# Output projection of an attention and MLP kernel: from full-array matmuls to two 64-row tiles, with new banks clearing and new queue orders

## The chip, the core and the metric

One NeuronCore of a Trainium2 chip. It has a matrix engine (TensorE, here PE), three elementwise engines (VectorE or DVE, ScalarE or ACT, GpSimd or POOL), a queue that issues transfers (SyncE or SP), on-chip memory of 128 partitions, and eight accumulator banks that only PE writes by matmul. Each engine takes its own instructions in order and waits on semaphores for the others. The metric is the device time of one execution, in microseconds (us); lower is better.

## The reference

Two layers, each an attention block A and an MLP block B on a sequence of 2048 tokens with 576 features; the same weights serve both layers. Cut to what matters:

```python
def _A_ref(x, wqkv, wo):            # H = 32 heads of Dh = 18, window W = 256
    q, k, v = split_heads(x @ wqkv)
    scores = einsum("bhqd,bhkd->bhqk", q, k) * Dh ** -0.5
    p = softmax(where(causal_and_within_W, scores, -1e9))
    o = einsum("bhqk,bhkd->bhqd", p, v)
    return merge_heads(o) @ wo      # the output projection, 576 x 576

def _B_ref(x, w1, b1, w2, b2):      # F = 4608
    h = gelu(layernorm(x) @ w1 + b1)
    return h @ w2 + b2

x = x + _A_ref(layernorm(x), wqkv, wo)
x = x + _B_ref(layernorm(x), w1, b1, w2, b2)
# and both once more
```

## The kernel before

**Tiling.** The two layers are cut into eight chunks of four token tiles (128 tokens each), four chunks a layer; `k` counts chunks from 0. For a chunk, PE runs: QKV (`qkv`, L842), scores (`scores`, L921, matmuls at L932), probabilities times values (`pv`, L966, matmuls at L978), the output projection (`tail`, L1051), the first MLP matmul (`G_part`, L1073, matmuls at L1098) and the second (`mm2`, L1120). ACT does the exponentials (L941) and the gelu (L1108), POOL the masks (L961), DVE the copies out of the banks, the layer-norm statistics (L719) and the residual adds (L1041). Work of neighbouring chunks is interleaved.

**Order.** Every piece of work is a task made by `add`, numbered in the order in which the program makes it. The order of the tasks on each of the five queues is not computed at build time: it is written out in the table `ORDER` (one string of task numbers for each engine), and the bank of every accumulator in the string `BANKS`. `Plan.schedule` walks through these strings with a cost for every task and puts in the waits; its one choice is to fill PE's gaps in the first 140 us with dummy matmuls (`keep_warm`, `warm_fn` at L709). The constant `SWITCH` is its cost for a change of array mode.

**Array shapes.** Every PE task has a mode. "f" uses the whole array. "r" (scores) uses four tiles of 32 rows. "c" uses either the whole array or four tiles of 32 columns (`quad`, L802: line 804 is the whole array, line 807 the four column tiles); `Plan.schedule` takes the column tiles where the task stands next to `pv`, which always uses them. "h" (QKV from the third chunk on, L863, and `G_part`) uses two tiles of 64 rows that write two different banks. An "h" task pair works in two phases: in the first, rows 0 to 63 write bank 0 and rows 64 to 127 write bank 1; in the second the halves change banks. Because both halves then add to what the other half wrote, the second phase is marked `own` and waits for PE's own count of the first. In the last of five pieces of features (`c == 4`, 64 features) QKV needs only the first phase, so the phases have ten and eight matmuls.

**Attention output.** Heads are kept in four groups of eight, one group in every 32 partitions; after `pv`, DVE transposes the result into `oq` (L989), divides by the sum into `attq` (L992, L995) and transposes `attq` into `attT` (L999) in five pieces of 32 columns, with task names `aT0` to `aT4`. A head group has 8 x 18 = 144 features, so pieces 0 to 3 hold 32 features of each group and piece 4 holds 16 features and 16 zeros. The zeros come from a POOL memset of `attq` (`aqd`) and a DVE memset of piece 4 of `wo_sb`.

**Output projection.** `tail` makes for each token tile two tasks by `two_out` (L811), one for each half of 288 output columns; each takes a bank and runs five matmuls, one for each piece, with `attT` against `wo_sb`. `resid` then adds each bank to the residual stream (L1041), and the layer norm for the MLP follows.

**Start and weights.** SP loads two tiles of x (`xin`), the weights of q (`wqA`, `wqB0`, `wqB1`), those of k and two more tiles of x. PE clears the eight banks by matmuls of a zeroed tile `warm` (`zero`, L697, L700), transposes the first tiles (L761) and starts on QKV of chunk 0 (L823). `wo_load` (L1202) issues four loads of 128 rows (`woA`) and four of 16 rows (`woB`).

Of the kernel before, what the change touches and what calls it, by code (L numbers as in the profile page):

```python
# [348 lines left out]
SWITCH = 0.103  # L349
# [4 lines left out]
def spread(s):  # L354
    for x in s.split():
# [178 lines left out]
def build_kernel(nc, A_x, A_wqkv, A_wo, B_x, B_w1, B_b1, B_w2, B_b2, out):  # L534
# [96 lines left out]
    def mm_cost(n):  # L631
        return n / 2400.0 + 0.0023
# [706 lines left out]
```

## Time and profile before

| | |
|---|---|
| Runs, median (lowest to highest of 3) | 860.43 us (859.88 to 860.76) |
| The profiled execution's own time | 860.22 us |
| Its span, first to last instruction | 858.5 us |
| Granted clock of PE over the span | 1.00 |
| Bytes read from HBM | 90.10 MB, 108 GB/s over the span |

The profile is one execution. "Busy" is the time in which an engine has at least one instruction running, "idle before" the time that an engine stood still just before the instructions of a group, with what ended it. A group is all instructions of one source line, engine and operation; `x` stands ahead of their number. A timeline merges neighbours of one group and gives the start, the length, and the group. Matmuls overlap: a new one starts before the last has ended, so a rate is read from start to start.

### The profile page before, as it was taken

Reading aid. Unit: us, or ns where it says so; the run is one execution under the profiler, and the core shown is the slowest. Engines: PE = TensorE matmul, PEld = TensorE weight load, DVE = VectorE, ACT = ScalarE, POOL = GpSimd, SP = SyncE. Lnnn points to the kernel's source line nnn. Section 1 sums busy time; section 2 is a strip of 40 time slices with the busy share of each in tenths; the row PEclk is TensorE's granted clock in tenths of the full one; section 3 lists DMA queues with packets and bytes.
Section 4 is the critical chain, followed back from the end, with each engine's and each line's share of the span. In section 5 each row is a group of like instructions: output and inputs, shape, how many; then the busy total and the mean of one; then the engine's idle time right before and its main releaser. Section 6 shows DMA issues by size and latency. Waiting matters only on the chain.

```text
span 858.5 us, 26755 instructions
## 1 busy us (share of the span) xinstructions
PE 846.7 (99%) x11500; PEld 521.2 (61%) x11500; DVE 384.8 (45%) x934; ACT 596.1 (69%) x741; POOL 371.3 (43%) x560
## 2 busy tenths in 40 slices
PE   8999999999999999999999999999999999999998
PEld 6555556656556566566566666756656656656556
DVE  6788234545237533373255632663325424243013
ACT  4986887868767788477755887548777689762730
POOL 3766644565235563156330672424634265421200
PEclk9999999999999999999999999999999999999999
DMA  7495763472575721956348626475444773535620
GB/s 210 75 164 118 225 184 92 123 197 55 161 177 120 157 75 61 209 145 173 94 133 205 164 63 211 69 162 146 133 131 91 157 226 100 161 128 141 232 84 28
DMA packets 181862, 119.77 MB, mean 140 GB/s; under 512 B 107440, under 2 KB 181744, under 8 KB 181744
## 3 DMA queue, kind: packets, MB, share of 16 engines
q1 hardware_dynamic: 181744, 118.05, 53.0%
q8 instruction: 91, 1.49, 0.7%
q14 instruction: 27, 0.22, 0.1%
HBM read 90.10 MB, written 2.36 MB: 108 GB/s over the span
## 4 chain that ended last, share of the span: by engine, by line
PE 93%; ACT 2%; issue 1%; DMA 1%; DVE 1%; POOL 1%; SPq 0%
PE ps L1098 33%; PE ps L804 30%; PE ps L863 10%; PE ps L807 8%; PE ps L932 6%; PE ps L978 5%; ACT pT L941 2%; PE ps L823 1%; POOL pT L961 1%; DMA wqkv<-in_A_wqkv_dram 1%; DMA xnTm<-xn 0%; SPq L659 0%; ACT hT L1108 0%; DVE oq L989 0%; DVE xn L744 0%
## 5 line engine op out<-in xcount | busy, mean ns | idle before, releaser
L941 ACT ACTIVATE pT<-ps 128x1024 bf16<-128x1024 f32 (+1 forms) x384 | 346.5, 972 | 62.4 <-PE ps L932 61.7
L961 POOL TENSOR_SCALAR_AFFINE_SELECT pT<-pT 128x512 bf16<-128x512 bf16 (+1 forms) x368 | 280.3, 785 | 238.7 <-ACT pT L941 233.9
L1098 PE MATMUL ps<-xnTm,w_sb 64*128 64x512 bf16 x2592 | 291.2, 376 | 1.4 <-DMA xnTm<-xn 0.5
L1108 ACT ACTIVATE hT<-ps,b1col 128x512 bf16<-128x512 f32 x276 | 169.5, 687 | 162.2 <-PE ps L1098 161.8
L1098 PEld LDWEIGHTS ps<-xnTm,w_sb 64*128 64x128 bf16 x2592 | 130.1, 94 | 141.1 <-issue 7.6
L804 PE MATMUL ps<-w_sb,hT 128*128 128x288 bf16 x1542 | 205.8, 287 | 0.0
L1041 DVE TENSOR_TENSOR x_res<-ps,x_res 128x288 f32<-128x288 f32 x224 | 98.3, 449 | 181.0 <-PE ps L804 159.1
L804 PEld LDWEIGHTS ps<-w_sb,hT 128*128 128x128 bf16 x1542 | 143.5, 98 | 52.2 <-issue 15.2
L863 PE MATMUL ps<-wqkv,xnTa 64*128 64x288 bf16 x1296 | 92.2, 283 | 0.9 <-DVE x_res L1041 0.3
L884 DVE CAST qn<-ps 128x288 bf16<-128x288 f32 x120 | 50.8, 448 | 83.6 <-PE ps L863 78.3
L989 DVE STREAM_TRANSPOSE oq<-ps 128x512 f32<-128x512 f32 x64 | 45.7, 714 | 93.3 <-PE ps L978 92.5
L863 PEld LDWEIGHTS ps<-wqkv,xnTa 64*128 64x128 bf16 x1296 | 62.0, 94 | 30.5 <-issue 3.8
L807 PE MATMUL ps<-w_sb,hT 128*32 128x288 bf16 x2280 | 79.2, 286 | 0.0
L807 PEld LDWEIGHTS ps<-w_sb,hT 128*32 128x32 bf16 x2280 | 58.7, 97 | 11.9 <-issue 3.3
L932 PE MATMUL ps<-qT,kT 32*128 32x384 bf16 (+2 forms) x1216 | 64.1, 276 | 1.2 <-ACT pT L941 1.2
L871 DVE CAST vA<-ps 128x288 bf16<-128x288 f32 x64 | 27.5, 449 | 74.6 <-PE ps L863 71.5
L732 POOL TENSOR_SCALAR vtmp<-mv_all 128x1 f32<-128x1 f32 (+1 forms) x43 | 8.5, 199 | 113.3 <-DVE mv_all L723 110.8
L719 DVE BATCH_NORM_STATS2 st_all<-x_res 128x6 f32<-128x288 f32 (+1 forms) x128 | 54.2, 445 | 3.3 <-DMA x_res<-in_A_x_dram 2.8
L1113 POOL TENSOR_TENSOR x_res<-x_res,b2bc 128x576 f32<-128x576 f32 x32 | 40.5, 1277 | 32.7 <-ACT hT L1108 32.7
L978 PE MATMUL ps<-pT,vA 128*20 128x384 bf16 (+2 forms) x1408 | 50.4, 276 | 0.8 <-DVE vA L871 0.6
L932 PEld LDWEIGHTS ps<-qT,kT 32*128 32x128 bf16 x1216 | 19.3, 92 | 41.7 <-issue 27.6
L804 PE MATMUL ps<-wo_sb,attT 128*128 128x288 bf16 x320 | 43.1, 287 | 0.2 <-issue 0.2
(56 smaller groups left out, 460.3 us busy)
## 6 DMA issues: line engine op xcount, KB each, us to landing
w_sb<-in_B_w_dram SPq DMA_DIRECT2D x46, 864.0 KB, 5.5
w_sb<-in_B_w_dram SPq DMA_DIRECT2D x48, 768.0 KB, 5.6
w_sb<-in_B_w_dram SPq DMA_DIRECT2D x96, 48.0 KB, 3.4
wqkv<-in_A_wqkv_dram SPq DMA_DIRECT2D x3, 576.0 KB, 5.4
x_res<-in_A_x_dram SPq DMA_DIRECT2D x3, 576.0 KB, 5.8
wqkv<-in_B_w_dram SPq DMA_DIRECT2D x2, 864.0 KB, 5.1
out_dram<-x_res SPq DMA_DIRECT2D x12, 144.0 KB, 3.2
wo_sb<-in_A_wo_dram SPq DMA_DIRECT2D x4, 144.0 KB, 2.6
```

What stands on the lines that cost most here:

```text
L719: add("dve", lambda e, i=i, s=s: e.bn_stats(st_all[:, t, i, :], s[:, t, i * HB:(i + 1) * HB]), reads=res, writes=[f"st{t}_{i}"], cost=0.37 ...
L804: return e.matmul(bank(b)[:, 0:HB], lhs, rhs, start=start, stop=stop, skip_group_check=True)
L807: ins = e.matmul(bank(b)[32 * j:32 * j + 32, 0:HB], lhs[:, 32 * j:32 * j + 32], rhs, start=start, stop=stop, tile_position=(0, 32 * j), sk ...
L863: ins = e.matmul(bank(bs[o])[:, 0:HB], xnTa[r:r + 64, c, i * 128:(i + 1) * 128], wqkv[r:r + 64, c, col:col + HB], start=(c == 4), stop=(ph ...
L884: add("dve", lambda e, b=bs[o], dst=dst: e.tensor_copy(dst, heads_of(bank(b))), reads=[bs[o]], writes=[f"qn{sl}h{o}"], cost=0.375, lat=0.1 ...
L932: ins = e.matmul(two(bs[j // 2])[:, j % 2, col:col + nq * 128], k_of(T0 + so)[0][32 * j:32 * j + 32, g, :], qs[32 * j:32 * j + 32, g, qo * ...
L941: add("act", lambda e, h2=h2: e.activation(pT[:, sl, 2 * h2:2 * h2 + 2, lo:hi], two(bs[h2])[:, :, lo:hi], ACT.Exp, scale=SCALE), reads=[bs ...
L961: add("pool", lambda e, ap=ap, pat=pat, sgn=sgn, kind=kind: e.affine_select(ap, ap, pattern=pat, compare_op=(ALU.is_ge if kind == "d" else ...
L978: ins = e.matmul(bank(bo)[32 * j:32 * j + VW, qo * 128:(qo + nq) * 128], vA[:, (T0 + so) % VS, 8 * j + g, :], pT[:, sl, j, col:col + nq * ...
L1041: add("dve", lambda e: e.tensor_tensor(x_res[:, t, sl], bank(b)[:, 0:HB], x_old[:, t, sl], ALU.add), reads=[b] + ([f"xin{t}"] if first els ...
L1098: ins = e.matmul(bank(bks[i])[:, 0:n], w1_sb[r:r + 64, sls[i], col:col + 128], xnTm[r:r + 64, k % 2, c, 0:n], start=(c == 4), stop=(ph == ...
L1108: add("act", lambda e, ff=ff, hd=hd, bk=bk: e.activation(hd[:, 0:n], bank(bk)[:, 0:n], ACT.Gelu_apprx_tanh, bias=b1col[:, ff:ff + 1]), rea ...
```

## The change

- **Projection.** `tail` makes for each token tile two tasks of mode "h" with two banks: ten matmuls in the first phase, then eight with `own`, each of 64 rows.
- **Packing.** After the last head group of a chunk, two DVE copies (`ax0`, `ax1`) write columns 128 to 143 of partitions 0 to 63 into columns 144 to 159 of partitions 64 to 127, and the other way round. After the transpose, either half of piece 4 holds the last 16 features of all four groups, in 64 rows. `wo_load` puts the matching weights there: the lower 64 rows for the first 288 columns, the upper 64 for the other, by eight loads of 16 rows and 288 columns instead of four of 16 rows and 576. The two memsets for zeros go.
- **Clearing.** Eight tasks of two 256-column matmuls on the whole array become one task of 35 matmuls of 512 columns in tiles of 64 x 128, 32 x 128, 128 x 32 and 32 x 64 (rows x columns).
- **Order.** `ORDER` and `BANKS` are replaced as a whole; `SWITCH`, and the transfer rate that the planner assumes, change. The second PE transpose of a first tile now names both of its sources.

```diff
-SWITCH = 0.103
+SWITCH = 0.110
...
-        n = 2 if cls != "xr" else 4
+        n = 2
...
-        kw.setdefault("move", n / (330e3 if cls != "xr" else 165e3))
+        kw.setdefault("move", n / 280e3)
...
-    add("pool", lambda e: e.memset(attq[:, :, 8 * DH:KD * 32], 0.0), writes=["aqd"], cost=0.5, prio=-8)
...
-    add("dve", lambda e: e.memset(wo_sb[:, 4, :], 0.0), writes=[f"woB{j}" for j in range(4)], cost=0.4, prio=-8)
...
-    def zero(e, b):
+    def zero(e, bs):
+
         ins = None
-        for c in range(2):
-            ins = e.matmul(bank(b)[:, c * 256:(c + 1) * 256], warm[:, :], warm[:, :].unsqueeze(1).to_broadcast([P, 2, P]), start=True, stop=True)
+        row = [[(0, 64, 0, 0, 128), (64, 64, 1, 0, 128)]] + [[(0, 64, 0, 0, 128), (64, 32, 2, 0, 128), (96, 32, 3, 0, 128)]] * 3
+        col = [[(0, 128, 4, 64 * h, 32), (0, 128, 4, 64 * h + 32, 32)] + [(32 * j, 32, (5, 6, 7, 0)[j], 64 - 64 * h, 64) for j in range(4)] for h in (0, 1, 0, 1)]
+        for tiles in (*row, *col):
+            for r, nr, b, c, ncol in tiles:
+                ins = e.matmul(bank(bs[b])[c:c + ncol, :], warm[r:r + nr, 0:ncol], warm[r:r + nr, :].unsqueeze(1).to_broadcast([nr, 4, P]),
+                               start=True, stop=True, tile_position=(r, c), skip_group_check=True)
         return ins
-    for i in ZERO:
-        b = Bank((i,))
-        add("pe", lambda e, b=b: zero(e, b), reads=["warm"], writes=[b], cost=0.43, lat=0.2, prio=-7, alloc=[b])
+    zs = [Bank((i,)) for i in range(8)]
+    add("pe", lambda e: zero(e, zs), reads=["warm"], writes=zs, cost=3.5, lat=0.2, prio=-7, alloc=zs)
...
-                add("pe", fn, reads=rd[cs[0] // 4:][:1] + ["ident"], writes=[b], cost=0.1 * len(cs), prio=prio, alloc=[b] if cs[0] == 0 else ())
+                add("pe", fn, reads=rd[:1 + cs[0] // 4] + ["ident"], writes=[b], cost=0.1 * len(cs), prio=prio, alloc=[b] if cs[0] == 0 else ())
...
+        if g == G - 1:
+            for h in range(2):
+                add("dve", lambda e, h=h: e.tensor_copy(attq[64 - 64 * h:128 - 64 * h, 0:4 * nt, 144:160], attq[64 * h:64 * h + 64, 0:4 * nt, 128:144]),
+                    reads=[f"aq{g}"], writes=[f"ax{h}"], cost=0.33, lat=0.14, prio=prio - 3)
...
-                    reads=[f"aq{x}" for x in range(32 * c // DH, g + 1)] + ["aqd"], writes=[f"aT{c}"], cost=0.6, lat=0.14, prio=prio - 3)
+                    reads=[f"aq{x}" for x in range(32 * c // DH, g + 1)] + (["ax0", "ax1"] if c == KD - 1 else []), writes=[f"aT{c}"], cost=0.6, lat=0.14, prio=prio - 3)
...
-            bs = two_out(lambda c, i=i: attT[:, c, i * 128:(i + 1) * 128], lambda c, s: wo_sb[:, c, s:s + HB],
-                         [f"aT{c}" for c in range(KD)] + [f"wo{x}{j}" for x in "AB" for j in range(4)], prio, mode="c")
+            bs = [Bank(FILL), Bank(FILL)]
+            for ph in range(2):
+                def half(e, ph=ph, i=i, bs=bs):
+                    ins = None
+                    for c in ((4, 0, 1, 2, 3) if ph == 0 else (0, 1, 2, 3)):
+                        for o in ((0, 1) if ph == 0 else (1, 0)):
+                            r = 64 * (o ^ ph)
+                            ins = e.matmul(bank(bs[o])[:, 0:HB], attT[r:r + 64, c, i * 128:(i + 1) * 128], wo_sb[r:r + 64, c, o * HB:o * HB + HB],
+                                           start=(c == 4), stop=(ph == 1 and c == 3), tile_position=(r, 0), skip_group_check=True)
+                    return ins
+                add("pe", half, reads=[f"aT{c}" for c in range(KD)] + [f"woA{j}" for j in range(4)] + [f"woB{n}" for n in range(8)], writes=bs,
+                    cost=mm_cost(HB) * (5 - ph), lat=0.22, prio=prio, mode="h", own=(ph == 1), alloc=(bs if ph == 0 else ()))
...
-            dma("sp", wo_sb[32 * j:32 * j + 16, 4, :], A_wo[r + 128:r + 144, :], reads=["aq0"], writes=[f"woB{j}"], cls="wo", cost=0.6)
+        for n, j in enumerate((0, 2, 1, 3, 2, 0, 3, 1)):
+            r = 8 * DH * j + 128
+            cols = slice(n // 4 * HB, n // 4 * HB + HB)
+            dma("sp", wo_sb[16 * n:16 * n + 16, 4, cols], A_wo[r:r + 16, cols], reads=["aq0"], writes=[f"woB{n}"], cls="wo", cost=0.6)
```

The first task numbers of PE and SP show how far the start moves (12 on each; 0 and 1 are the first tiles of x, 2 to 4 the weights of q, 5 to 7 those of k, 8 two more tiles of x, 9 to 11 the weights of v):

```diff
 "pe":
-        "27 31 29 33 26 28 32 30 43 44 77 83
+        "24 34 35 69 68 48 49 74 73 84 58 59
...
 "sp":
-        "0 2 1 4 3 5-8 76 10 11
+        "0 2 1 6 3 8 4 7 5 67 10 9
```

In the new numbering 24 is the clearing, 34 and 35 transpose the first tile, 68 and 69 are its q, 48 and 49 transpose the second tile, 73 and 74 are the k of the first.

More of the change, by code (lines that the diff above doesn't have):

```diff
@@ L361 @@
     "pe":
[47 rows of a table removed]
-    "act":
[30 rows of a table removed]
-    "dve":
[37 rows of a table removed]
-    "pool":
[39 rows of a table removed]
[49 rows of a table added]
+    "act":
[30 rows of a table added]
+    "dve":
[38 rows of a table added]
+    "pool":
[39 rows of a table added]
 }
 BANKS = (
-        "76543210313512070747601020376160667676414240244240524627402460240240274024026402470240240250202407676676707766667677"
-        "76767571654460202020240202026042077456310275420420420472042047204213766766710264503751642042042004203076765677567544"
-        "67546754675675467625646767210654702312040020452002204202056767746765473104410320060240724020240204576435676723601137"
-        "54602402402740245766076466527574765467554752437266575675271501623546702020240624020270202547675436654712360123020240"
-        "24702402450202447676767465762305703202402406240216767752447655446572554764147757472654566066341074031020202025040202"
-        "40204764674776623017456320202024027402402340246676747667012564710320240240274024236767267314545566457704742656574556"
-        "27646076301233705202002040200424524207671667574765234076230420204270420427042076736667646230165431202020202602023573"
-        "56754747465754675754665567456202316470123560714230204204250442204202477656766770162345602302022024702402450202667456"
-        "76746570123012302400402640242573677645674764675717646574257456746747136510132467502022440642042034204176267656230176"
-        "74526042042042604204260420667766777645723016457202042027202064654765714741603675430172603511207543417203460122604753"
-        "14567301265737416531704351467230757234130")
@@ new lines @@
+        "76543210636216464741055501616364445433750226600620162626402470420422604262461264206246246242002631610100454671110150"
+        "01077742574650424020260220201624247632407163542060206042606203622637545454550324176514060026026526623254140455410767"
+        "63276657465745410415342531576405301700660060276202207242455424457616073461071020602606526022042020445547745653274106"
+        "53202620620660047454573255432767564647574745326654324763273624710754002060424704240262040757676766547362307162024204"
@@ new lines @@
+        "20640200272020167564767643012750375642464262462411710106075642121302147656420523076547632357631745310200440423024004"
+        "52020377627676107463254376064606466044040364044323222722105524376760626062610220253746445743240524352653076256043425"
+        "35342506161725741066002602260606706027532445457465321076542024246402464260422466175010164107573524104040404704040376"
+        "72761762763716076736263306532620574512174647521300242042450242027202036767647664757532641040640460046644226446133221"
@@ L534, in build_kernel @@
+        "10331205476326464246426646263010147155764304765326375216250274162505442651337417362462660504060600606643322501764253"
+        "20536124024202440200252002776577667647510327564206202624626235450544134714236517640415250157672306075433421642760651"
+        "45170643251045647106360754260431542673571")
 def build_kernel(nc, A_x, A_wqkv, A_wo, B_x, B_w1, B_b1, B_w2, B_b2, out):
@@ L617, in build_kernel @@
     OUT = (7, 6, 5, 4)
-    ZERO = (7, 6, 5, 4, 3, 2, 1, 0)
     MM1 = (0, 1, 2, 3, 4, 5, 6, 7)
```

307 rows, old and new, of the table ORDER are left out of this document.

## The prediction

> **What bounds the kernel now.** I read the page first, then the list of waits of TensorE (PE).
>
> ```profile
> span 858.5 us, 26755 instructions
> PE 846.7 (99%) x11500; PEld 521.2 (61%) x11500; DVE 384.8 (45%) x934; ACT 596.1 (69%) x741; POOL 371.3 (43%) x560
> PEclk9999999999999999999999999999999999999999
> ```
> ```profile
> PE ps L700 <- DVE warm L695: 1.6, 1, 1.6
> PE ps L823 <- DMA wqkv<-in_A_wqkv_dram: 1.6, 1, 1.6
> PE ps L932 <- ACT pT L941: 1.5, 7, 0.2
> PE ps L978 <- DVE vA L871: 0.6, 1, 0.6
> PE ps L1098 <- DMA xnTm<-xn: 0.5, 1, 0.5
> ```
>
> PE is busy for 99% of the span at full clock, and no other engine passes 69%. The five longest waits make 5.8 us; 3.2 us of them (L700, L823) lie in the first ten microseconds. So the time is the length of PE's own instruction stream plus a few waits. Columns taken off that stream shorten the kernel one for one, as long as the hand-written order leaves no new hole in it.
>
> "Busy" doesn't tell how fast PE streams, because matmuls overlap. I take rates from start to start, in the timeline of PE where the fifth chunk's QKV, first MLP matmuls and output projection follow each other (start, length, then the group):
>
> ```profile
> 459.18 0.78 PE L863 MATMUL ps<-wqkv,xnTa 64*128 64x288 bf16 x10
> 459.79 1.24 PE L1098 MATMUL ps<-xnTm,w_sb 64*128 64x512 bf16 x10
> 460.87 0.65 PE L863 MATMUL ps<-wqkv,xnTa 64*128 64x288 bf16 x8
> 461.36 1.03 PE L1098 MATMUL ps<-xnTm,w_sb 64*128 64x512 bf16 x8
> ...
> 467.63 2.62 PE L804 MATMUL ps<-wo_sb,attT 128*128 128x288 bf16 x20
> 470.19 0.40 PE L932 MATMUL ps<-qT,kT 32*128 32x384 bf16 x8
> 470.52 0.79 PE L804 MATMUL ps<-wo_sb,attT 128*128 128x288 bf16 x5
> 471.14 1.63 PE L804 MATMUL ps<-w_sb,hT 128*128 128x288 bf16 x12
> ...
> 537.98 1.52 PE L863 MATMUL ps<-wqkv,xnTa 64*128 64x288 bf16 x18
> 539.43 0.91 PE L804 MATMUL ps<-w_sb,hT 128*128 128x288 bf16 x6
> ...
> 545.84 2.38 PE L863 MATMUL ps<-wqkv,xnTa 64*128 64x288 bf16 x36
> 548.15 0.40 PE L932 MATMUL ps<-qT,kT 32*128 32x256 bf16 x8
> ```
>
> **Term 1, the projection itself.** Today five 128-row matmuls of 288 columns take 471.14 - 470.52 = 0.62 us, and two whole token tiles with one change of array shape behind them 470.19 - 467.63 = 2.56 us. With about 0.10 us for the change (next paragraph) that is 1.23 us for a tile's ten matmuls. The new form issues ten 64-row matmuls, then eight: exactly what L863 does for QKV with the same 288 columns. There ten take 459.79 - 459.18 = 0.61 us and eight 461.36 - 460.87 = 0.49 us, together 1.10 us, because two of them run at a time (a pair in 0.122 us). Ten slots become nine: 0.125 us less for each tile, and there are
>
> ```profile
> L804 PE MATMUL ps<-wo_sb,attT 128*128 128x288 bf16 x320 | 43.1, 287 | 0.2 <-issue 0.2
> ```
>
> 320 / 10 = 32 tiles: **-4.0 us**.
>
> **Term 2, changes of array shape.** The projection moves from the full array to the 64-row shape, which QKV and the first MLP matmul use. A change costs (548.15 - 545.84) - 2 x 1.10 = 0.11 us, some 0.10 us. I counted shapes along both PE order strings of the diff (task numbers shifted by the tasks that the diff adds and removes): 414 changes before, 413 after. Projection tiles sit more often next to 64-row work, but scores (32-row) are cut into it as often: **-0.1 us**.
>
> **Term 3, the second phase waits for the first.** The second eight matmuls carry the wait that QKV has (`own`): the row halves swap banks, so PE waits for its own count. Where nothing stands between the phases, QKV's eighteen take 539.43 - 537.98 = 1.45 us, less 1.10 and a change of 0.10: 0.25 us of emptying. In the new order, 6 of the 32 tiles have their phases directly behind each other; the other 26 have another matmul task in between, the shortest a score group with 0.33 us (470.52 - 470.19), which covers 0.25 us. QKV has 6 such places instead of 5. Seven times 0.25: **+1.75 us**. Queued behind each such wait is all of PE.
>
> **Term 4, the packing copies.** Two copies on DVE for each chunk, sixteen in all, each of 256 bf16 per partition on 64 partitions, stand between the last group's normalisation and the transpose of piece 4 (`aT4`), for which the first projection matmul waits. No row has this copy; the nearest are
>
> ```profile
> L884 DVE CAST qn<-ps 128x288 bf16<-128x288 f32 x120 | 50.8, 448 | 83.6 <-PE ps L863 78.3 <-PE ps L807 2.2 <-PE ps L804 2.1
> L1218 DVE CAST b1col<-ps 128x36 f32<-128x36 bf16 x1 | 0.2, 186 | 0.0
> ```
>
> so between 0.19 and 0.45 us; I take 0.32, between them, 0.64 us for the two (0.38 to 0.90). In four chunks only the PE work of 4 to 6 tasks covers that chain; the others have 5.8 us and more. The transposes beside the first projection matmul, in the first and the sixth chunk:
>
> ```profile
> 64.93 1.30 DVE L999 STREAM_TRANSPOSE attT<-attq 128x512 bf16<-128x512 bf16 x2
> 66.91 2.00 PE L804 MATMUL ps<-wo_sb,attT 128*128 128x288 bf16 x15 [0.20 <-issue]
> ...
> 554.58 1.30 DVE L999 STREAM_TRANSPOSE attT<-attq 128x512 bf16<-128x512 bf16 x2
> 556.61 1.63 PE L804 MATMUL ps<-wo_sb,attT 128*128 128x288 bf16 x12
> ```
>
> Slack from the transposes' end: 66.91 - 66.23 = 0.68 and 556.61 - 555.88 = 0.73 us, each above 0.64; the last chunk has more. In the third (k = 2) the new order takes a residual add out of the chain and puts one more score group on PE. **0 us**; at 0.90 us for a pair 0.2 us shows in each of these two chunks, and without any cover four chunks would pay 4 x 0.64 = 2.6 us.
>
> **Term 5, the start.** Rows of PE and of DVE:
>
> ```profile
> 1.63 3.37 PE L700 MATMUL ps<-warm 128*128 128x256 bf16 x16 [1.63 <-DVE warm L695]
> 5.68 0.51 PE L761 MATMUL ps<-ident,xn 128*128 128x128 bf16 x5 [0.35 <-DVE xn L744]
> 7.01 0.77 PE L823 MATMUL ps<-wqkv,xnTa 128*128 128x288 bf16 x5 [0.28 <-ACT xnTa L764]
> 9.37 1.39 PE L823 MATMUL ps<-wqkv,xnTa 128*128 128x288 bf16 x10 [1.58 <-DMA wqkv<-in_A_wqkv_dram]
> 9.85 0.82 DVE L719 BATCH_NORM_STATS2 st_all<-x_res 128x6 f32<-128x288 bf16 x2 [0.94 <-DMA x_res<-in_A_x_dram]
> ```
>
> Clearing streams 16 x 256 = 4096 columns in 3.4 us (the first matmuls run slowly). The new clearing has 35 matmuls of 512 columns, grouped so that eight groups fill the array side by side: 8 x 512 = 4096 columns, the same 3.4 us, and the first transpose waits for DVE until 5.68 anyway. After it PE now does both halves of the first q and the second transpose before the first k; the load for k is queued behind two more tiles of x. The nine loads were all in at 9.85, so k starts there instead of at 9.37 (+0.48), but 0.61 us of q and some 0.27 us of transpose are done by then: **-0.4 us**. Bounds: -0.9 (k still at 9.37) and +0.5 (nothing gained). The last weight rows come in eight small loads instead of four:
>
> ```profile
> L659 SPq DMA_DIRECT2D wo_sb<-in_A_wo_dram x8: 347/504/588, 34.4 to 62.0; - x8
> ```
>
> Four more at 0.5 us (the median of min/median/max in ns) hold up SP, and the transposes queued on it, by 2 us between 34 and 62 us; all twelve stand there ahead of the last k transpose of their stretch, while the old last one stood behind it. The two memsets that go were beside other work. Nothing booked for either.
>
> **Sum.** -4.0 - 0.1 + 1.75 - 0.4 = -2.75 us: the span of 858.5 becomes 855.75. The median of the runs, 860.43, lies 1.93 above the span (the profiled execution's own time is 860.22), so I forecast **857.7 us**. What no row prices is the search: every queue is re-sorted. I value it at 0 for the likeliest case, with -2.6 and +2.6 as bounds: the three waits of the list behind the start (1.5 + 0.6 + 0.5) all gone, or as much again.
>
> **Rivals.**
> *The new order also closes holes:* no wait after the start, 857.7 - 2.6 = **855.1**. For it: 1.5 us of PE's waits are seven small ones on the exponentials, a matter of spacing. Against it: the old order was searched too.
> *The new order opens holes:* 857.7 + 2.6 = **860.3**. For it: all queues move at once, so every cover of the old order is up for change. Against it: the list is short for 11500 matmuls, so orders with few waits can be found.
> *The mixed clearing doesn't overlap.* Nothing in the trace runs tiles of two sizes side by side. All 35 one after the other: eight at 3.4/8 = 0.42 us, then 27 at 0.216 us (460.87 - 459.79 for five) = 9.2 us, the end at 10.8; plus 1.33 us to q (7.01 - 5.68), 1.23 and 0.27, so k starts near 13.6 instead of 9.85: +3.8, **861.5**, slower than before. If only different sizes exclude each other there are 15 groups and 14 changes: 3.4 + 7 x 0.216 + 1.4 = 6.3 us, k at 10.8, +0.9: 858.6. The kernel becomes slower once clearing ends after about 9.7. [...]
> *The residual adds become the wait.* A tile now keeps two of four banks until both adds have run, and both become ready at once:
>
> ```profile
> L1041 DVE TENSOR_TENSOR x_res<-ps,x_res 128x288 f32<-128x288 f32 x224 | 98.3, 449 | 181.0 <-PE ps L804 159.1 <-PE ps L807 21.0
> L719 DVE BATCH_NORM_STATS2 st_all<-x_res 128x6 f32<-128x288 f32 x96 | 41.4, 447 | 0.4
> ```
>
> Two adds are 0.90 us, a tile on PE 1.10. One statistic of 0.45 us queued between them makes it 1.35, and the tile after next is 0.25 us late; with both, 0.70 us. It decides where it catches 4 of the 32 tiles (2.75 / 0.70); caught on one tile in five, 6.5 x 0.70 = 4.5 us: **862.2**. Against it: the order can put scores and statistics between, and DVE is idle half the time.
> *The pairs don't overlap:* 18 x 0.122 = 2.2 us a tile, +31 us, **889**. L863 has the very shape; nearly excluded.
>
> **How the numbers follow.** Forecast 0.55 (own range 856.4 to 859.2), holes closed 0.17, holes opened 0.08, clearing 0.10, adds 0.09, no overlap 0.01. Less than 0.2% (1.7 us, about what a measurement tells from nothing) is no change: faster means under 858.7, slower over 862.1. Faster: 0.48 of the forecast, 0.17 of the holes closed and 0.03 of the clearing (its smaller form), **0.68**. Same: 0.07 of the forecast, 0.08 and 0.06 of the holes opened and the clearing, **0.21**. Slower: 0.09, 0.01 and 0.01 of the adds, the clearing and no overlap, **0.11**. The range goes from 855.1 less the 0.5 of the start's lower bound, 854.6, to the clearing's 861.5; the adds, the last case and the edges stay outside.
>
> **What would show it.** Term 1: 576 matmuls of 64 rows with `wo_sb`, ten in 0.61 us. Term 3: tiles with eighteen in a row of 1.35 us. Term 4: no PE wait on `attT`. Term 5: clearing ends by 5.1 and k starts near 9.85. I am wrong if PE's list of waits grows by several microseconds, above all on DVE's adds or on ACT, or if clearing reaches past 7 us.

## The result and the profile after

The changed kernel is slower. Eight runs of each:

| | median (lowest to highest) | profiled execution: own time, span |
|---|---|---|
| before | 860.51 us (859.88 to 861.92) | 860.22, 858.5 us |
| after | 862.77 us (862.11 to 863.81) | 863.81, 862.1 us |

The ratio is 1.0026, 95% interval 1.0015 to 1.0037: +2.3 us, where -2.75 was forecast. The profiled execution is the longest of the eight, so the accounts below are made against its own span, +3.6 us.

The page of the changed kernel, its span and the busy time of the engines:

```profile
span 862.1 us, 27852 instructions
PE 848.2 (98%) x12042; PEld 517.9 (60%) x12042; DVE 387.3 (45%) x949; ACT 597.3 (69%) x741; POOL 371.4 (43%) x559
```

and its list of PE's waits (total, times, longest), the answer to the first list of the prediction:

```profile
PE ps L704 <- DVE warm L695: 2.3, 1, 2.3
PE ps L1116 <- DMA xnTm<-xn: 2.3, 3, 1.3
PE ps L936 <- issue: 1.2, 1, 1.2
PE ps L936 <- ACT pT L945: 1.0, 4, 0.3
PE ps L808 <- DVE qn L888: 0.8, 2, 0.5
PE ps L1116 <- DVE qn L888: 0.6, 1, 0.6
```

PE is still the bound, and nothing stands on the residual adds (the one row on them, L1071, has 0.2 us). But the list behind the start, all rows added and those of clearing and the first QKV left out, has grown from 4.1 to 6.8 us. The start, in the timeline of PE:

```profile
2.31 7.68 PE L704 MATMUL ps<-warm 64*128 64x512 bf16 x35 [2.31 <-DVE warm L695]
9.92 0.45 PE L765 MATMUL ps<-ident,xn 128*128 128x128 bf16 x5
...
12.70 2.00 PE L827 MATMUL ps<-wqkv,xnTa 128*128 128x288 bf16 x15
...
34.06 0.67 PE L982 MATMUL ps<-pT,vA 128*20 128x384 bf16 x16
```

Clearing takes 7.7 us instead of 3.4 and reaches to 10.0. It also starts 0.68 us later (2.31 instead of 1.63), because the new order of DVE puts the memset of `warm` behind three others (0.42, 0.17 and 0.42 us) instead of two (0.17 and 0.42). The first transpose starts at 9.92 instead of 5.68, the first k at 12.70 instead of the forecast 9.85. The first `pv` is a good mark because the whole start lies ahead of it. In the kernel before it is

```profile
32.18 0.67 PE L978 MATMUL ps<-pT,vA 128*20 128x384 bf16 x16 [0.19 <-POOL pT L961]
```

so the changed kernel is 34.06 - 32.18 = 1.9 us late there. The projection of the fifth chunk, in its timeline further on:

```profile
467.95 0.79 PE L1071 MATMUL ps<-wo_sb,attT 64*128 64x288 bf16 x10
468.56 0.67 PE L867 MATMUL ps<-wqkv,xnTa 64*128 64x288 bf16 x8
...
470.60 2.62 PE L1071 MATMUL ps<-wo_sb,attT 64*128 64x288 bf16 x36
473.15 0.40 PE L936 MATMUL ps<-qT,kT 32*128 32x384 bf16 x8
473.48 0.66 PE L1071 MATMUL ps<-wo_sb,attT 64*128 64x288 bf16 x8
474.07 0.91 PE L808 MATMUL ps<-w_sb,hT 128*128 128x288 bf16 x6
```

Ten matmuls take 468.56 - 467.95 = 0.61 us, eight with the change behind them 474.07 - 473.48 = 0.59, so 0.49: a tile is 1.10 us, as forecast. The 36 in a row take 2.55 us: two tiles, a change and one emptying of 2.55 - 2.20 - 0.10 = 0.25 us. The rows of the projection and of the packing copies among the groups (busy, mean ns | idle before):

```profile
L1071 PE MATMUL ps<-wo_sb,attT 64*128 64x288 bf16 x576 | 41.1, 283 | 0.7 <-DVE x_res L1049 0.2
L1003 DVE COPY attq<-attq 64x256 bf16<-64x256 bf16 x16 | 3.5, 222 | 0.5
```

From each start of a projection group to the start of what follows, listed idle time left out, PE spends 40.7 us on the projection before and 39.0 after, changes of shape and emptying behind its groups included.

### The profile page after: what moved, and what is told of

Its sections match the earlier page's. It is cut to its first block, busy times and chain, and to the rows that moved or that the text cites. A ratio compares the mean times of both kernels' runs of the same rounds, so it can differ in the third digit from the quotient of the medians.

```text
span 862.1 us, 27852 instructions
## 1 busy us (share of the span) xinstructions
PE 848.2 (98%) x12042; PEld 517.9 (60%) x12042; DVE 387.3 (45%) x949; ACT 597.3 (69%) x741; POOL 371.4 (43%) x559
## 4 chain that ended last, share of the span: by engine, by line
PE 92%; DMA 4%; ACT 2%; DVE 1%; issue 1%; SPq 0%; DVEq 0%
PE ps L1116 32%; PE ps L808 25%; PE ps L811 10%; PE ps L867 9%; PE ps L936 6%; PE ps L982 4%; PE ps L1071 4%; DMA xnTm<-xn 2%; ACT pT L945 1%; PE ps L827 1%; PE ps L704 1%; DMA x_res<-qn 1%; DMA kT<-qn 1%; DVE qn L888 0%; DMA xnTa<-xn 0%
## 5 line engine op out<-in xcount | busy, mean ns | idle before, releaser
L808 PE MATMUL ps<-w_sb,hT 128*128 128x288 bf16 x1452 | 193.9, 287 | 0.2 <-DVE oq L993 0.2
L808 PEld LDWEIGHTS ps<-w_sb,hT 128*128 128x128 bf16 x1452 | 134.4, 98 | 50.9 <-issue 15.2
L811 PE MATMUL ps<-w_sb,hT 128*32 128x288 bf16 x2640 | 91.7, 287 | 0.0
L811 PEld LDWEIGHTS ps<-w_sb,hT 128*32 128x32 bf16 x2640 | 67.7, 97 | 15.0 <-issue 5.3
L936 PEld LDWEIGHTS ps<-qT,kT 32*128 32x128 bf16 x1216 | 19.4, 92 | 40.7 <-issue 24.8
L1071 PE MATMUL ps<-wo_sb,attT 64*128 64x288 bf16 x576 | 41.1, 283 | 0.7 <-DVE x_res L1049 0.2
L748 DVE TENSOR_SCALAR xn<-x_res,mv_all,rstd 128x576 bf16<-128x576 f32 (+1 forms) x64 | 36.6, 578 | 10.8 <-DMA xnTm<-xn 4.3
```

Of the source, the lines that this page charges most:

```text
L808: return e.matmul(bank(b)[:, 0:HB], lhs, rhs, start=start, stop=stop, skip_group_check=True)
L811: ins = e.matmul(bank(b)[32 * j:32 * j + 32, 0:HB], lhs[:, 32 * j:32 * j + 32], rhs, start=start, stop=stop, tile_position=(0, 32 * j), sk ...
L936: ins = e.matmul(two(bs[j // 2])[:, j % 2, col:col + nq * 128], k_of(T0 + so)[0][32 * j:32 * j + 32, g, :], qs[32 * j:32 * j + 32, g, qo * ...
L1071: ins = e.matmul(bank(bs[o])[:, 0:HB], attT[r:r + 64, c, i * 128:(i + 1) * 128], wo_sb[r:r + 64, c, o * HB:o * HB + HB], start=(c == 4), s ...
```

## The experiments

Two questions. What does each of the three parts (clearing, projection, order) cost by itself? And why is the clearing slow? All ratios of experiments are against runs of the kernel before on the same chip. A trace is of one execution, and executions of one kernel differ by up to 5 us (857.8 to 862.8 us in the first experiment), so the cost of a part is read from the runs, and the trace tells where it may lie.

**The old clearing in the changed kernel.** The clearing goes back to the whole array, as one task; all else stays.

```diff
-        for tiles in (*row, *col):
-            for r, nr, b, c, ncol in tiles:
-                ins = e.matmul(bank(bs[b])[c:c + ncol, :], warm[r:r + nr, 0:ncol], ..., tile_position=(r, c))
+        for b in range(8):
+            for c in range(2):
+                ins = e.matmul(bank(bs[b])[:, c * 256:(c + 1) * 256], warm[:, :], ...)
```

> The changed kernel with one thing undone: the banks are cleared by sixteen 256-column matmuls on the whole array again; all queue orders stay new. Theory A (the mixed clearing runs one tile size at a time and delays the start of PE's real work for good): clearing ends near 2.3 + 3.4 = 5.7 us instead of 9.9, k starts at about 9.9 (its weights) instead of 12.7, the first probabilities-times-values group at 32.2 to 32.8 instead of 34.06, and the time falls by 1.3 to 2.0 us, to 860.8 to 861.5. Rival B (start waits for weights anyway, the loss is made by the new order behind the first 60 us): the time stays at 862.5 to 863.0.

Measured: 859.62 us, ratio 0.9994 (0.9984 to 1.0004). Its timeline of PE:

```profile
2.31 3.59 PE L702 MATMUL ps<-warm 128*128 128x256 bf16 x16 [2.31 <-DVE warm L695]
5.83 0.71 PE L762 MATMUL ps<-ident,xn 128*128 128x128 bf16 x5
...
10.36 2.01 PE L824 MATMUL ps<-wqkv,xnTa 128*128 128x288 bf16 x15 [0.93 <-DMA wqkv<-in_A_wqkv_dram]
...
31.73 0.67 PE L979 MATMUL ps<-pT,vA 128*20 128x384 bf16 x16
```

The first `pv` is now 0.45 us earlier than in the kernel before: in this execution the reordered start is worth the 0.4 us that it was given. Theory A has the place right and the size too small, as the time is 1.2 us under its range. The mixed clearing costs 1.0026 - 0.9994 = 0.32%, 2.8 us, of which 34.06 - 31.73 = 2.3 us are seen at the first `pv`. Without it the kernel can't be told from the one before: the projection's gain is missing too.

**The mixed clearing alone.** The kernel before, with the 35 matmuls as one task in the place of the eight clearing tasks.

```diff
-    for i in ZERO:
-        b = Bank((i,))
-        add("pe", lambda e, b=b: zero(e, b), ..., cost=0.43, lat=0.2, prio=-7, alloc=[b])
+    zs = [Bank((i,)) for i in range(8)]
+    add("pe", lambda e: zero(e, zs), ..., cost=3.5, lat=0.2, prio=-7, alloc=zs)
```

> The kernel before with the mixed clearing as the only edit (one task in place of eight, at the same place in PE's order). Theory A: clearing lasts 7.6 us as in the changed kernel and ends near 9.2, the first q starts near 10.6 instead of 7.0, later work is delayed by 1.5 to 2.2 us, the time is 862.0 to 862.7. Rival B: under 0.5 us of it is left at 60 us, the time is 860.3 to 861.0.

Measured: 864.25 us, ratio 1.0045 (1.0033 to 1.0058). Its timeline:

```profile
1.63 8.16 PE L703 MATMUL ps<-warm 64*128 64x512 bf16 x35 [1.63 <-DVE warm L694]
...
35.07 0.67 PE L981 MATMUL ps<-pT,vA 128*20 128x384 bf16 x16 [0.19 <-POOL pT L964]
```

Alone, the clearing costs 0.45%, 3.9 us, more than theory A allowed. The profiled execution is the slowest of the five, with a span 5.4 us above that of the kernel before: 35.07 - 32.18 = 2.9 us stand at the first `pv`, and the waits of the same old order behind the start grow from 4.1 to 6.7 us. Of these rows the first had 0.5 us before and the second is new:

```profile
PE ps L1101 <- DMA xnTm<-xn: 2.1, 2, 1.7
...
PE ps L1101 <- DVE oq L992: 0.6, 1, 0.6
```

So a late start is paid once at the start. In this execution new waits for transposes come on top; that the shift makes them is not shown.

**One size of clearing tile.** The changed kernel with 32 matmuls of 512 columns, all in tiles of 128 x 32, four side by side.

```diff
+        for b in range(8):
+            for j in range(4):
+                ins = e.matmul(bank(bs[b])[32 * j:32 * j + 32, :], warm[:, 0:32], ..., tile_position=(0, 32 * j))
```

> The changed kernel, its orders and projection, with the clearing made of one tile size: 32 matmuls of 512 columns in 128 x 32 tiles, four side by side per bank (35 matmuls in four sizes before). Theory A (tiles of different size don't run side by side, and each change of size empties the array): eight groups of four at 0.43 us, 3.4 us in all, the end near 5.8, and the time as with the whole-array clearing, 2.4 to 3.2 us under the changed kernel: ratio to the kernel before 0.9985 to 1.0005. Rival D (many tile instructions in the clearing are slow whatever their size): clearing stays near 7 us and the ratio near 1.0026.

Measured: 859.82 us, ratio 0.9990 (0.9981 to 1.0000). Its clearing:

```profile
2.31 3.60 PE L702 MATMUL ps<-warm 128*32 128x512 bf16 x32 [2.31 <-DVE warm L695]
```

Almost as many small matmuls of the same length, side by side, cost what the whole array costs (3.60 against 3.59 us). The 4 us are the price of neither small tiles nor many instructions.

**The same 35 matmuls, sorted by size.** The weight loads of the changed kernel's clearing (PEld, start and length) show what the array does:

```profile
2.30 0.13 PEld L704 LDWEIGHTS ps<-warm 64*128 64x128 bf16 x3 [2.30 <-DVE warm L695]
3.27 0.10 PEld L704 LDWEIGHTS ps<-warm 32*128 32x128 bf16 x2 [0.84 <-issue]
3.81 0.10 PEld L704 LDWEIGHTS ps<-warm 64*128 64x128 bf16 x1 [0.44 <-issue]
...
8.71 0.13 PEld L704 LDWEIGHTS ps<-warm 32*64 32x64 bf16 x4 [0.43 <-issue]
9.25 0.10 PEld L704 LDWEIGHTS ps<-warm 128*32 128x32 bf16 x2 [0.41 <-issue]
9.57 0.11 PEld L704 LDWEIGHTS ps<-warm 32*64 32x64 bf16 x4 [0.23 <-issue]
```

Where the size changes, the next loads come 0.54 to 0.57 us later (3.27, 3.81), whichever half of the array is free, until 9.25; the last step is 0.32. 512 columns at the rate of the old clearing are 3.59/8 = 0.45 us, and the weight loads of the one-size clearing come in steps of 0.43 (3.13, 3.56, 3.99 us), so a step is one round plus 0.11 us of change. The kernel of this experiment issues all matmuls of one size together:

```diff
-        row = [[(0, 64, 0, 0, 128), (64, 64, 1, 0, 128)]] + [[(0, 64, 0, 0, 128), (64, 32, 2, 0, 128), (96, 32, 3, 0, 128)]] * 3
...
-        for tiles in (*row, *col):
-            for r, nr, b, c, ncol in tiles:
+        row = [(0, 64, 0, 0, 128), (64, 64, 1, 0, 128)] + [(0, 64, 0, 0, 128)] * 3 + [(64, 32, 2, 0, 128), (96, 32, 3, 0, 128)] * 3
+        col = [(0, 128, 4, 64 * h + 32 * q, 32) for h in (0, 1, 0, 1) for q in range(2)]
+        col += [(32 * j, 32, (5, 6, 7, 0)[j], 64 - 64 * h, 64) for h in (0, 1, 0, 1) for j in range(4)]
+        for r, nr, b, c, ncol in row + col:
```

> The changed kernel with the same 35 clearing matmuls of 512 columns, issued size by size: five of 64x128, six of 32x128, eight of 128x32, sixteen of 32x64. Theory S (only tiles of one size run side by side, and each change of size empties the array): the tile positions now allow 4 + 3 + 2 + 2 = 11 rounds at 0.43 us and 3 changes at 0.11 us, 5.1 us, so the clearing group shows 5.0 to 5.3 us instead of 7.68, the first transpose starts near 7.5 instead of 9.92, and the ratio to the kernel before falls from 1.0026 to about 1.000 (within 0.0015). Rival M (the price is per matmul, 35 at 0.22 us, whatever their order): 7.7 us again, the first transpose near 9.9, ratio 1.0026. Rival B (rounds as before, 15, and only the changes are saved): 15 x 0.43 + 3 x 0.11 = 6.8 us, first transpose near 9.1.

Measured: 861.31 us, ratio 1.0012 (1.0001 to 1.0022). Its timeline of PE, then of the weight loads:

```profile
2.31 5.25 PE L704 MATMUL ps<-warm 64*128 64x512 bf16 x35 [2.31 <-DVE warm L695]
7.50 0.71 PE L765 MATMUL ps<-ident,xn 128*128 128x128 bf16 x5
...
32.07 0.67 PE L982 MATMUL ps<-pT,vA 128*20 128x384 bf16 x16
```

```profile
4.12 0.13 PEld L704 LDWEIGHTS ps<-warm 32*128 32x128 bf16 x4 [0.84 <-issue]
...
5.51 0.14 PEld L704 LDWEIGHTS ps<-warm 128*32 128x32 bf16 x8 [0.84 <-issue]
6.48 0.20 PEld L704 LDWEIGHTS ps<-warm 32*64 32x64 bf16 x16 [0.83 <-issue]
```

The same 35 matmuls take 5.25 us: eleven rounds and three changes (5.1 expected), not the 7.7 of a price per matmul nor the 6.8 of unchanged rounds. Sixteen 32 x 64 tiles in eight positions load within 0.20 us and are through in two rounds (7.49 - 6.48). So in these loads tiles of one size run side by side at every position that the clearing uses, and in no step do tiles of two sizes run together. This settles where the clearing's time goes, and by what mechanism: rounds of equal tiles at 0.43 us each, and some 0.11 us for a change of size between them, within one task and even where the next tile's rows stand free.

**The old projection in the changed kernel.** `tail` goes back to `two_out` on the whole array, with the zeros of piece 4 of `wo_sb` written by a DVE memset; mixed clearing and new order stay. The packing copies stay as well, with zeros around the packed rows of the weights.

```diff
-            bs = [Bank(FILL), Bank(FILL)]
-            for ph in range(2):
...
-                add("pe", half, ..., mode="h", own=(ph == 1), alloc=(bs if ph == 0 else ()))
+            bs = two_out(lambda c, i=i: attT[:, c, i * 128:(i + 1) * 128], lambda c, s: wo_sb[:, c, s:s + HB], ..., mode="f")
```

> The changed kernel, orders and clearing and packing copies as they are, but each projection tile again as two tasks of five whole-array matmuls (piece 4 with zero weights in the rows of the other half; the zeros come from one DVE memset near 25 us). Theory A (the two-tile projection does what was forecast: -4.0 us of streaming, +1.5 us for six tiles with their phases back to back): 2.5 us slower than the changed kernel, 865.2. Rival C (the new order is waiting for other engines often enough that PE's columns don't count): within 0.7 us of the changed kernel, 862.1 to 863.5.

Measured: 864.47 us, ratio 1.0049 (1.0036 to 1.0062), between the two theories and nearer to A. By the ratios the 64-row projection in place is worth 1.0049 - 1.0026 = 0.23%, 2.0 us; the intervals just touch. The profiled spans differ by 1.0 us (863.1 and 862.1), and all of that stands at the first `pv` already (35.10 against 34.06), up to which both versions run the same matmuls: here the slow rate of the start lasts longer (last section), and clearing takes 8.15 us.

```profile
2.31 8.15 PE L704 MATMUL ps<-warm 64*128 64x512 bf16 x35 [2.31 <-DVE warm L695]
```

Its list of waits is shorter (3.7 us behind the start, against 6.8):

```profile
PE ps L1112 <- DVE xn L754: 1.4, 1, 1.4
PE ps L942 <- ACT pT L951: 1.0, 4, 0.3
```

**The new order alone.** The edits of the first experiment and of the one just above together: old clearing, whole-array projection, new order.

> The changed kernel with the old clearing and the whole-array projection: what is left of the change are the new queue orders, the packing copies and loads. Theory E (the new order opens holes of 1 to 2.5 us of its own against the old one, which eat what the projection brings): ratio to the kernel before 1.0012 to 1.0030 (861 to 862.6 where before is 860.0). Rival F (the orders are worth the same, and the projection brings less than 1 us): ratio 0.9995 to 1.0008.

Measured: 861.10 us, ratio 1.0012 (1.0003 to 1.0021). The profiled execution is one of the fastest of the eleven (860.26 us); its span of 858.5 us is that of the kernel before. Its waits behind the start are fewer (2.7 us against 4.1):

```profile
PE ps L939 <- ACT pT L948: 1.0, 4, 0.3
...
PE ps L814 <- issue: 0.6, 1, 0.6
```

So in this execution the order by itself opens no hole above 0.6 us: the ratio lies at the lower edge of theory E, but not for its reason. What the trace shows as a cost is that the order was written for a projection of 64 rows: with the whole array, PE changes its shape 433 times instead of 417 (counted along the order, dummy matmuls included; the kernel before has 418 by that count). Against the first experiment, which has the 64-row projection in the same order, this gives 0.18%, 1.5 us, for the projection; the intervals of the two overlap.

**Fewer column tiles beside `pv`.** One hole has no releaser. In the changed kernel's timeline:

```profile
504.38 3.85 PE L811 MATMUL ps<-w_sb,hT 128*32 128x288 bf16 x120
508.16 0.39 PE L936 MATMUL ps<-qT,kT 32*128 32x384 bf16 x7
509.77 0.21 PE L936 MATMUL ps<-qT,kT 32*128 32x128 bf16 x1 [1.22 <-issue]
```

Seven of eight score matmuls run, then PE waits 1.2 us for nothing that the profile shows. Ahead of it stand 120 column-tile matmuls; the kernel before runs this work, and that of the 24 just ahead of the `pv`, as 36 whole-array ones. The kernel of the first experiment has the hole too (1.0 us), that of the one-size clearing and the sorted one as well (1.5 each). Here `Plan.schedule` takes the whole array for runs of more than 3 us of planned cost beside a `pv` group, instead of 4; 28 tasks change their form, with six more changes of shape.

```diff
-                if not at or sum(x.cost for x in part) > 4.0:
+                if not at or sum(x.cost for x in part) > 3.0:
```

> The changed kernel with the old clearing, and the bound from which a run of second-MLP tasks beside a probabilities-times-values task uses the whole array lowered from 4.0 to 3.0 us of planned cost: 28 tasks of 24 column-tile matmuls become 28 of 6 whole-array matmuls, among them the five in a row ahead of 507 us; six more changes of array shape (+0.6 us). Theory G (PE runs dry there because 144 small matmuls with their weight loads come in 5 us and the instructions behind them aren't fetched in time): the hole of 1.2 to 1.5 us with no releaser near 507 us is gone, and the time falls by 0.5 to 1.0 us against the same kernel without it (ratio to before 0.9982 to 0.9990 where that had 0.9994). Rival H (the hole sits at a place in the instruction stream, whatever the tiles): the hole stays or moves, and the ratio is 1.0000 to 1.0006.

Measured: 859.24 us, ratio 0.9990 (0.9981 to 0.9999). At that place:

```profile
501.06 3.85 PE L805 MATMUL ps<-w_sb,hT 128*128 128x288 bf16 x30
504.84 0.40 PE L933 MATMUL ps<-qT,kT 32*128 32x384 bf16 x8
```

The same work takes the same 3.85 us, with a quarter of the matmuls, and this execution has no hole there. The whole time can't be told from the first experiment's (0.9994), so the gain of theory G is not shown, and neither is its cause, the fetching of instructions; the six changes, at 0.105 us each (0.10 to 0.11 by the rows of the projection and of QKV), would take back some 0.6 us. With the one-size clearing this is the lowest ratio found, 0.1% under the kernel before, at the edge of what the interval can tell.

**The order moved again.** The kernel of the first experiment, with its strings improved by single moves against the costs that `Plan.schedule` writes down: at least 134 of 1198 PE tasks and 320 of 949 DVE tasks at another place, tasks of the other three queues too, 102 of 1201 banks chosen anew; by those costs 1.2 us shorter.

> The changed kernel with the old clearing, and its orders and banks improved by single moves against the same planner's costs with 0.097 us for a change of shape. What is tested is whether the holes of the new order can be closed by hand. Theory E (the holes between 36 and 66 us and near 486 us are made by the order): planner's gain is 1.2 us, so ratio to before 0.9978 to 0.9988. Rival I (the holes come from transfers that land late by chance, which no order of the planner sees): ratio 0.9990 to 1.0002.

Measured: 875.31 us, ratio 1.0173 (1.0159 to 1.0187), 15 us slower, and neither of the times expected. Its waits behind the start make 19.0 us, spread over 19 rows:

```profile
PE ps L934 <- ACT pT L943: 4.5, 9, 1.2
PE ps L1114 <- ACT hT L1124: 2.5, 2, 1.5
```

An order that is 1.2 us shorter by the written costs is 15 us longer on the chip, so at this level these costs can't tell a good order from a bad one. Which of its moves made the waits is not known.

No run has the new projection in the old order, which was not written for a tile that holds two banks until both adds have run. So what the projection does without the new order stays open.

## Why the prediction was wrong

The profiled spans, taken apart against the kernel before (us). "First pv" is its start less 32.18; "projection" is PE's time on it as above, less 40.7; "QKV" one more emptying of 0.25; "shapes" the changes beyond those in the projection's groups, at 0.105 (16 more in the two whole-array versions, of which 1.0 us stands already under projection; six in the last); "waits" the sum of the list behind the start less 4.1.

| kernel | first pv | projection | QKV | shapes | waits | sum | span |
|---|---|---|---|---|---|---|---|
| after | +1.9 | -1.8 | +0.25 | 0 | +2.7 | +3.1 | +3.6 |
| old clearing | -0.45 | -1.8 | +0.25 | 0 | +1.2 | -0.8 | -0.6 |
| mixed clearing alone | +2.9 | 0 | 0 | 0 | +2.6 | +5.5 | +5.4 |
| one size | +0.6 | -1.7 | +0.25 | 0 | +2.2 | +1.4 | +1.3 |
| sorted | -0.1 | -1.7 | +0.25 | 0 | +1.5 | -0.1 | +0.3 |
| old projection | +2.9 | +1.0 | +0.25 | +0.7 | -0.4 | +4.5 | +4.6 |
| order alone | -0.5 | +1.0 | +0.25 | +0.7 | -1.4 | 0.0 | 0.0 |
| fewer column tiles | +0.1 | -1.7 | +0.25 | +0.6 | 0.0 | -0.75 | -0.4 |

The account closes within 0.6 us for each. It is one of single executions: "after" and "old projection" run the same matmuls up to the first `pv` and differ by 1.0 us there. By the steps of the prediction:

**Term 1, -4.0: right in its rate.** 1.10 us a tile, as forecast, in 576 matmuls. With the emptyings it makes -2.5; the rows show -1.8. Three more of the projection's groups end in a change of shape than before (17 against 14), 0.3 us, and one further second phase starts 0.16 us late; some 0.2 us I can't place.

**Term 2: right.** 417 changes against 418 by the count above.

**Term 3, +1.75: right.** 6 tiles and 6 QKV pairs have their phases directly behind each other, each with about 0.23 us of emptying (0.35 us from the last start of the first phase to the next, less the 0.12 of a pair), 2.8 us in all against 1.2 before: +1.6.

**Term 4, 0: right.** A copy is 0.22 us, under the 0.32 taken, and no row has PE waiting for `attT`.

**Term 5: the step that failed.** "Grouped so that eight groups fill the array side by side, the same 3.4 us" is false. Sorting the same matmuls by size took 2.4 us off, one size alone another 1.7. The mechanism stood as a rival, with 15 groups and 14 changes. Its price was too low: 6.3 us against 7.68, because I let only the first eight rounds run at the slow rate of the start. The loads show 0.54 us a step until 9.25, 6.9 us after PE's first matmul. With all rounds at the slow rate 15 x 0.43 + 14 x 0.11 = 8.0 us, and the two executions in which it lasted beyond clearing show 8.15 and 8.16. And by its own late k (10.8) the rival's time was 858.6; the first k came at 12.70. The size of the reordering, -0.4, is not settled: it took k's weights as landed at 9.85, and in the four versions with a clearing of 3.6 us (new order alone, old clearing, fewer column tiles, one size) the last of them lands at 10.0, 10.3, 10.9 and 11.4, and the first `pv` comes 0.5 and 0.45 us earlier and 0.1 and 0.6 us later than in the kernel before.

**The search, valued at 0: the second step that failed.** Its bound of +2.6 is what the list of waits shows, +2.7, but that is luck: the bound was the sum of three old waits, and the new ones stand at other places. It isn't the order by itself, which has 1.4 us less of waits than the old one with the whole-array projection. In both pairs that differ in the projection alone the waits grow with the 64-row form: from 2.7 to 5.3 us with the old clearing, from 3.7 to 6.8 with the mixed one; the other three with the 64-row form in this order have 4.1 to 6.3. These are traces of one execution each. In them the 4 us that the projection saves are given back as 1.4 us of emptying in its own rows and some 3 us of waits for transposes, for DVE and for the next instruction. That PE simply reaches the same transposes sooner is a reading that I have not tested. Single holes move: the wait on `xnTm` is 2.3 us in the changed kernel, 1.8 with the one-size clearing and under 0.5 with the sorted one, in the same order.

**The rivals.** "Opens holes" and the mixed clearing happened together, and I had priced each alone: 2.6 and 0.9 to 3.8 us on top of -2.75. On the account of the spans the changed kernel has +2.3 us of clearing and -0.4 of reordered start at the first `pv`, -1.8 for the projection, +0.25 for QKV and +2.7 of waits, 3.05 of the 3.6. All 35 clearing matmuls one after the other came closest by its time (861.5), but the sorted clearing's 5.25 us rules its mechanism out. The residual adds never became a wait, and the pairs do overlap. "Wrong if clearing reaches past 7 us" was the sign to look at: it reaches 10.0.

## What to carry to other kernels

In these traces array tiles run side by side only while they have one size (35 matmuls in 7.68 us mixed, 5.25 sorted), so count rounds of equal tiles and a change of about 0.11 us between sizes, never columns, and sort small tiles by size. Time taken from the bounding engine in small pieces can be given back at once: here, in the traces, 4 us of shorter matmuls came back as 1.4 us of emptying and some 3 us of waits. Change the order, the shape and the start in separate kernels first; the start was legible alone and not from the sum.

## What was not expected of the hardware

**The start is slow, and for how long differs.** The first matmuls run at half the later rate: 256 columns from start to start take 0.213 us, later 0.11. Dummies of 256 columns show until when, in the timelines of the kernel before (two lines), of the old clearing, of the changed kernel and of the old projection:

```profile
4.84 0.49 PE L709 MATMUL ps<-warm 128*128 128x256 bf16 x3
6.02 0.71 PE L709 MATMUL ps<-warm 128*128 128x256 bf16 x5
6.34 1.27 PE L710 MATMUL ps<-warm 128*128 128x256 bf16 x5
10.21 0.71 PE L713 MATMUL ps<-warm 128*128 128x256 bf16 x5
10.90 1.24 PE L713 MATMUL ps<-warm 128*128 128x256 bf16 x5
```

At the full rate five take 0.71 us and three 0.49, so (0.71 - 0.49)/2 = 0.11 each; at the slow one 9.07 - 8.00 = 1.07 us pass from the start of five to the start of what follows with the sorted clearing, and 11.29 - 10.23 = 1.06 with the mixed clearing alone, so 0.213 each. In the kernel before PE is fast at 6.02, and the three dummies at 4.84, 3.2 us after its first matmul, have the same rate. With the old clearing the last slow dummy starts 6.34 + 4 x 0.213 - 2.31 = 4.9 us after PE's first matmul. In the changed kernel the slow rate ends at 6.9 us. With the old projection, whose start is the same as the changed kernel's, the last slow dummy starts at 9.4 us.

The column of the granted clock doesn't show it. The changed kernel in a stretch of its start (us; busy us and number of PE, PEld, DVE, ACT, POOL; clock; share of DMA; GB/s):

```profile
4.30:6.30 2.00, 2.00 (x8) 0.41 (x7) 0.75 (x2) 0.24 (x1) 0.98 (x4) 1.00 1.05 349
```

The clock is given as 1.00 where 512 columns take 0.43 us. What sets the length of the slow phase, up to 3.2 us in the kernel before and up to 9.4 in the old projection, is not shown. So work at the start has a range of prices, and one trace gives only one of them.

**PE can stand still with no releaser.** The hole of 1.0 to 1.5 us behind the column-tile matmuls appears in four profiled executions, all with the 64-row projection, and not in the one where they are a quarter as many. At that place the two versions with the whole-array projection and the new order run the same 120 column-tile matmuls in the same 3.85 us without it (the order alone has a smaller one, 0.6 us, at another place), so their number alone is not the condition; why the next instruction comes late stays open.
